# Value halves of the U rounds of batches 0 and 1 in the PSUM banks of the output tiles

## The chip, the cores and the metric

The kernel runs on one core of one Trainium2 chip. The metric is the device time of the whole kernel in microseconds, as the median of several runs; lower is better. A run counts as slow when it lies over 1.5% above the fastest of the same kernel; all runs compared here are fast ones unless it is said otherwise. The runs were made in several batches, each on another chip, with the kernel before measured beside them every time. The granted clock is the share of TensorE's full clock that the chip's throttle let through. The profile is one further look at one execution; its span is some 1.8 us below the timed figure, and its times are counted from the span's start.

## The reference, cut to what matters

```python
# attention with 32 memory slots per head, 8 batches, 8 heads, 576 tokens
a = softmax(phi, over tokens)
k_m, v_m = a^T k, a^T v                       # per head: 32 x 64
attn = softmax(q k_m^T / 8)                   # 576 x 32
x = (attn v_m), heads side by side            # 4608 x 512
# gated feed-forward, 512 -> 1536 -> 512
out = (silu(x w_gate) * (x w_val)) w_out
```

The kernel never forms x. Since x w = attn (v_m w), it first multiplies the small v_m into the weights. That product is U, one for gates and one for values, per batch and per block of 512 columns ("chunk").

## The kernel before: the parts that matter

The kernel uses eight banks of PSUM, the memory to which TensorE writes its results; each tile takes one bank until ScalarE or VectorE has read it out. Six form the pool `ps`, from which nearly every tile comes; two form the pool `po` for output tiles (and for the dummy matmuls of `warm`).

```python
ps = ctx.enter_context(tc.tile_pool(name="ps", bufs=6, space=bass.MemoryType.PSUM))
po = ctx.enter_context(tc.tile_pool(name="po", bufs=2, space=bass.MemoryType.PSUM))
```

A U round computes one or two "parts" (in a full round the gate half and the value half of a chunk), each into two banks, and evacuates them to SBUF, alternately by ScalarE ("a") and VectorE ("v").

```python
def u_round(b, parts, evac):
    banks = []
    for which, c, halves in parts:
        ...
        p = [ps.tile([128, 2, HC], FP32, tag="b", name=f"p_u{g}")... for g in range(NG)]
        for w in which:
            for i in range(NP):
                for g in range(NG):
                    nc.tensor.matmul(p[g][32 * i:32 * i + 32, o:o + n], lhsT=kTs[b]..., rhs=W[w, c]...)
        ...
    for (t, p, r), e in zip(banks, evac):
        ...   # ScalarE: copy or activation; VectorE: tensor_copy or tensor_scalar
```

A gate and value slot computes a gate tile (two matmuls), has ScalarE take its silu, computes the value tile of the slot before (two matmuls), and has VectorE multiply the two. In batches 0 and 1 the slots and U rounds are in this order:

```python
run([u_half(1, (0, 1), 0, 1, "av")] + g0[4:8] + g1[4:5])
for c in range(1, NCH):                     # two chunks, so four full U rounds
    s = 8 * c
    run([u_item(0, c)] + g1[s - 3:s] + g0[s:s + 5])
    run([u_item(1, c)] + g0[s + 5:s + 8] + g1[s:s + 5])
run(g1[-3:])
flush_mul()
backlog = out_list(0) + out_list(1)         # po's banks: unused from the last warm to here
```

The softmax here doesn't subtract the row's maximum and nothing guards it: scores larger than these inputs give would overflow.

Of the kernel before, what the change touches and what calls it, by code (L numbers as in the profile page):

```python
# [9 lines left out]
FP32 = mybir.dt.float32  # L10
# [4 lines left out]
def kernel(  # L15
# [40 lines left out]
    ps = ctx.enter_context(tc.tile_pool(name="ps", bufs=6, space=bass.MemoryType.PSUM))  # L56
    po = ctx.enter_context(tc.tile_pool(name="po", bufs=2, space=bass.MemoryType.PSUM))
# [57 lines left out]
    HC = CH // 2  # L115
# [249 lines left out]

    scaled = set()

    def u_round(b, parts, evac):


        banks = []
        for which, c, halves in parts:
            w0, w1, h0, h1 = which[0], which[-1] + 1, halves[0], halves[-1] + 1
            n = (h1 - h0) * HC
            p = [
                ps.tile([128, 2, HC], FP32, tag="b", name=f"p_u{g}").rearrange("p a f -> p (a f)")
                for g in range(NG)
            ]
            for w in which:
                o = (w - w0) * n  # L380
                for i in range(NP):
                    for g in range(NG):
                        nc.tensor.matmul(  # L383
                            p[g][32 * i:32 * i + 32, o:o + n],
                            lhsT=kTs[b][64 * g:64 * g + 64, 2, 32 * i:32 * i + 32],
                            rhs=W[w, c][64 * g:64 * g + 64, h0:h1, i],
                            start=True,
                            stop=True,
                            tile_position=(64 * g, 32 * i),
                        )  # L390
            for g in range(NG):
                if (b, c, g) not in Us:
                    Us[b, c, g] = upool.tile([128, 2, 2, HC], BF16, tag=f"U{c}{g}", name="t_U")
                if len(which) == 1:
                    dst = Us[b, c, g][:, h0:h1, w0]
                else:
                    dst = Us[b, c, g][:, h0]
                src = p[g][:, 0:(w1 - w0) * n].rearrange("p (a f) -> p a f", f=HC)
                banks.append((dst, src, rSs[b][:, g, 0] if b in scaled else None))
        for (t, p, r), e in zip(banks, evac):  # L400
            if e == "a":
                if r is None:
                    nc.scalar.copy(out=t, in_=p)  # L403
                else:
                    nc.scalar.activation(out=t, in_=p, func=AF.Copy, scale=r)
            elif r is None:
                nc.vector.tensor_copy(out=t, in_=p)  # L407
            else:
                nc.vector.tensor_scalar(out=t, in0=p, scalar1=r, scalar2=None, op0=ALU.mult)
# [5 lines left out]
    def flush_mul(n=None):  # L415
        for _ in range(len(pend) if n is None else n):
            pend.pop(0)()
# [16 lines left out]
    def gv_gate(b, s):  # L434

        jf, r = s // 2, s % 2
        if b % 2 == 0 and r == 0:
            hts[b // 2, jf] = hpool.tile([128, 2 * S], BF16, tag=f"h{jf}", name="t_h")
        gate = gv_half(b, s, 0)
        sg = work.tile([128, HALF], BF16, tag="sg", bufs=8, name="t_sg")  # L440
        nc.scalar.activation(out=sg, in_=gate, func=AF.Silu)  # L441
        col = (b % 2) * S + r * HALF
        dst = hts[b // 2, jf][:, col:col + HALF]

        def mul():
            val = gv_half(b, s, 1)
            nc.vector.tensor_tensor(out=dst, in0=sg, in1=val, op=ALU.mult)  # L447

        pend.append(mul)
# [97 lines left out]
            lambda g=g, n=n: q_T(b, g, n, evac[2 * g + n]) for g in range(NG) for n in range(2)  # L547
        ]

    def u_item(b, c, evac="avav"):  # L550

        return lambda: u_round(b, (((0,), c, (0, 1)), ((1,), c, (0, 1))), evac)

    def u_half(b, which, c, half, evac):

        return lambda: u_round(b, ((which, c, (half,)),), evac)

    def u_three(b):

        u_round(b, (((0,), 0, (0, 1)), ((1,), 0, (0, 1)), ((0,), 1, (0, 1))), "avavav")  # L560
# [4 lines left out]
    def run(items):  # L565
        for x in items:
            x()
# [13 lines left out]
    def gv_slots(b):  # L581
        return [lambda s=s: gv_slot(b, s) for s in range(2 * NJF)]
# [78 lines left out]

    g0, g1 = gv_slots(0), gv_slots(1)
    run([u_half(0, (0,), 0, 0, "av"), u_half(1, (0,), 0, 0, "av")])
    warm(6)
    for s in range(4):
        gv_gate(0, s)
    run([u_half(0, (1,), 0, 0, "va"), u_half(1, (1,), 0, 0, "va")])
    for s in range(2):
        gv_gate(1, s)
    flush_mul(3)  # L670
    run([u_half(0, (0, 1), 0, 1, "va")])
    flush_mul(2)
    run(g1[2:4])
    run([u_half(1, (0, 1), 0, 1, "av")] + g0[4:8] + g1[4:5])
    for c in range(1, NCH):
        s = 8 * c
        run([u_item(0, c)] + g1[s - 3:s] + g0[s:s + 5])
        run([u_item(1, c)] + g0[s + 5:s + 8] + g1[s:s + 5])
    run(g1[-3:])
    flush_mul()  # L680
    backlog = out_list(0) + out_list(1)
# [7 lines left out]
    for b in range(2, B):  # L689
# [30 lines left out]
        g = gv_slots(b)  # L720
# [3 lines left out]
        if last:  # L724
            streams += [([u_item(b, 2)], 5, 6)]
# [55 lines left out]
```

## Time and profile before

The kernel took 249.45 us (249.39 to 249.8). The stages that the argument touches:

| stretch of the profile, us | what runs | what it waits for |
|---|---|---|
| 27 to 35.7 | half U rounds, first slots | U evacuations as data |
| 35.75 to 57.0 | four full U rounds, eight slots after each but the last, eleven after that | 0.3 us per round: banks in the second to fourth, mostly a load in the first (shown below) |
| 57.0 to 79 | output tiles of batches 0 and 1, K and V sums of batch 2 | nothing of note |
| 86.1 | K and V sums of batch 3 | nothing: V of batch 3 had landed at 85.5 |
| to 243.9 | batches 3 to 7 and the last output tiles | next to nothing |

A line of the chain of waits reads: start, length, engine, tile that is written, source line, number of instructions. A line of the timeline adds the operation and, in brackets, the engine's idle time before it and what ended that. The prediction below shows the lines of before.

### The profile page before, as it was taken

The page shows a single profiled execution, that of the slowest core. Times are in us where ns is not written, and L with a number is a line of the kernel's source. Part 1 is how long each engine was busy: PE and PEld are TensorE (multiplying, and loading weights), DVE is VectorE, ACT ScalarE, POOL GpSimd, SP SyncE. Part 2 cuts the span into 40 slices and gives each one's busy share as a digit, 9 for nine tenths or more (in the row PEclk, how much of TensorE's full clock was granted, in tenths as well). Part 3 has the DMA queues.
Part 4 walks back from the last instruction along what each step waited for, and adds up shares of the span by engine and source line. Part 5 has one row for each costly group of instructions (what it writes and reads, how often), then busy time and mean ns, then how long its engine had stood idle before and what let it go on. Part 6 is the DMA issues. An engine that isn't in the chain of part 4 may idle for free.

```text
span 247.6 us, 6587 instructions
## 1 busy us (share of the span) xinstructions
PE 237.5 (96%) x2573; PEld 152.3 (61%) x2600; DVE 158.9 (64%) x337; ACT 165.2 (67%) x356; POOL 54.5 (22%) x85
## 2 busy tenths in 40 slices
PE   7999999999999999999999999999999999999993
PEld 7966666665544765467645666476546655467543
DVE  0046599994437788479846778478846877587420
ACT  2447888886077667966896577966896577676201
POOL 8423455000060004060405420090007000000000
PEclk9999999999999999999999999999999999999998
DMA  7999999999689976996996599289425311310143
GB/s 182 206 204 203 196 197 201 233 199 198 134 158 248 231 168 95 207 282 145 125 243 191 94 175 249 91 119 196 94 51 123 65 42 42 87 42 0 45 128 85
DMA packets 49167, 37.00 MB, mean 149 GB/s; under 512 B 15984, under 2 KB 43888, under 8 KB 49136
## 3 DMA queue, kind: packets, MB, share of 16 engines
q0 software_dynamic: 27632, 22.42, 57.0%
q1 hardware_dynamic: 20496, 13.37, 22.7%
q10 hardware_dynamic: 1008, 0.79, 1.2%
q8 instruction: 20, 0.33, 0.5%
q14 instruction: 11, 0.09, 0.1%
HBM read 42.47 MB, written 9.44 MB: 210 GB/s over the span
## 4 chain that ended last, share of the span: by engine, by line
PE 87%; DMA 8%; POOL 2%; issue 2%; ACT 0%; POOLq 0%
PE p_oo L483 36%; PE p_g L425 20%; PE p_v L425 19%; DMA t_kv<-in_v_dram 8%; PE p_u L383 6%; PE p_kv L183 2%; PE p_oo L514 1%; POOL t_q L93 1%; POOL t_kv L81 1%; PE p_g L351 1%; PE p_v L351 1%; PE p_g L331 1%; PE p_vT L290 0%; PE p_kv L203 0%; PE p_oo L588 0%
## 5 line engine op out<-in xcount | busy, mean ns | idle before, releaser
L483 PE MATMUL p_oo<-WO,t_h 128*128 128x512 bf16 x393 | 101.6, 379 | 3.0 <-issue 2.9
L441 ACT ACTIVATE t_sg<-p_g 128x288 bf16<-128x288 f32 x192 | 76.9, 413 | 31.6 <-PE p_g L425 24.2
L447 DVE TENSOR_TENSOR t_h<-t_sg,p_v 128x288 bf16<-128x288 bf16 x192 | 84.3, 453 | 18.9 <-PE p_v L425 14.8
L425 PEld LDWEIGHTS <-t_U 128*128 128x128 bf16 x768 | 74.3, 98 | 30.7 <-issue 2.3
L425 PE MATMUL p_g<-t_A,t_U 128*128 128x288 bf16 x384 | 77.5, 286 | 0.4
L425 PE MATMUL p_v<-t_A,t_U 128*128 128x288 bf16 x384 | 76.8, 286 | 0.0
L483 PEld LDWEIGHTS <-t_h 128*128 128x128 bf16 x420 | 39.6, 98 | 41.0 <-issue 6.0
L495 DVE COPY t_o<-p_oo 128x512 f32<-128x512 f32 x27 | 18.6, 690 | 31.4 <-PE p_oo L483 31.3
L407 DVE CAST t_U<-p_u 128x512 bf16<-128x512 f32 x42 | 26.7, 684 | 6.8 <-PE p_u L383 6.8
L403 ACT CAST t_U<-p_u 128x512 bf16<-128x512 f32 x30 | 15.8, 592 | 8.9 <-PE p_u L383 8.9
L493 ACT COPY t_o<-p_oo 128x512 f32<-128x512 f32 x8 | 4.7, 589 | 19.9 <-PE p_oo L483 10.6
L100 POOL DMA_DIRECT2D t_q<-in_q_dram x6 | 4.7, 782 | 59.3 <-DMA t_qT<-t_q 58.5
L588 PE MATMUL p_oo<-bones 128*128 128x128 bf16 x198 | 15.7, 244 | 1.5 <-DVE bones L603 1.5
L383 PE MATMUL p_u<-W,t_kT 64*32 64x512 bf16 (+1 forms) x416 | 15.7, 365 | 0.1
L153 ACT ACTIVATE t_ephi<-t_phi 96x768 bf16<-96x768 f32 x16 | 12.5, 843 | 4.1 <-DMA t_phi<-in_phi_dram 4.1
L588 PEld LDWEIGHTS <-bones 128*128 128x128 bf16 x198 | 13.9, 111 | 2.1 <-DVE bones L603 1.5
L166 POOL COPY t_mark<-t_A 1x1 bf16<-1x1 bf16 x4 | 0.7, 181 | 55.7 <-DVE t_A L360 55.7
L341 ACT ACTIVATE t_E<-p_g 128x288 bf16<-128x288 f32 x16 | 6.6, 412 | 8.5 <-PE p_v L331 7.9
L360 DVE TENSOR_TENSOR t_A<-t_E,t_lz 128x576 bf16<-128x576 bf16 x16 | 11.5, 750 | 0.5 <-ACT t_lz L355 0.5
L355 ACT ACTIVATE t_lz<-t_lz 128x576 f32<-128x576 f32 x16 | 10.9, 684 | 0.5
L170 POOL TENSOR_TENSOR t_es<-t_es,t_ephi 96x256 f32<-96x256 f32 x16 | 10.7, 669 | 1.3
L383 PEld LDWEIGHTS <-t_kT 64*32 64x32 bf16 x416 | 4.8, 89 | 8.8 <-issue 7.3
(58 smaller groups left out, 167.9 us busy)
## 6 DMA issues: line engine op xcount, KB each, us to landing
t_kv<-in_k_dram POOLq DMA_DIRECT2D x8, 576.0 KB, 9.3
t_kv<-in_v_dram POOLq DMA_DIRECT2D x8, 576.0 KB, 14.2
out_dram<-t_o SPq DMA_DIRECT2D x23, 192.0 KB, 2.5
t_phi<-in_phi_dram POOLq DMA_DIRECT2D x6, 576.0 KB, 15.3
t_q<-in_q_dram POOLq DMA_DIRECT2D x6, 576.0 KB, 7.4
out_dram<-t_o SPq DMA_DIRECT2D x24, 128.0 KB, 2.5
W<-in_moe_w_gate_dram POOLq DMA_DIRECT2D x6, 256.0 KB, 12.9
W<-in_moe_w_val_dram POOLq DMA_DIRECT2D x6, 256.0 KB, 11.9
```

Source lines behind the costliest of these rows:

```text
L153: nc.scalar.activation(out=t[:, :, g].rearrange("p j i m -> p i j m"), in_=src[:, g], func=AF.Exp)
L355: nc.scalar.activation(out=lz, in_=lz, func=AF.Exp, scale=-1.0)
L360: nc.vector.tensor_tensor(out=a, in0=es.pop((b, g)), in1=lzs.pop((b, g)), op=ALU.mult)
L383: nc.tensor.matmul(p[g][32 * i:32 * i + 32, o:o + n], lhsT=kTs[b][64 * g:64 * g + 64, 2, 32 * i:32 * i + 32], rhs=W[w, c][64 * g:64 * g + ...
L403: nc.scalar.copy(out=t, in_=p)
L407: nc.vector.tensor_copy(out=t, in_=p)
L425: nc.tensor.matmul(p[:, 0:HALF], lhsT=Us[b, c, g][:, o // 2, which, 128 * (o % 2):128 * (o % 2 + 1)], rhs=atts[b, g][:, r], start=(g == 0) ...
L441: nc.scalar.activation(out=sg, in_=gate, func=AF.Silu)
L447: nc.vector.tensor_tensor(out=dst, in0=sg, in1=val, op=ALU.mult)
L483: nc.tensor.matmul(mine["p"], lhsT=hts[c, jf][:, 128 * u:128 * (u + 1)], rhs=WO[jf], start=(jf == 0), stop=(jf == NJF - 1),)
L495: nc.vector.tensor_copy(out=t_o, in_=mine["p"])
L588: nc.tensor.matmul(p[:, 0:128], lhsT=bones, rhs=bones, start=True, stop=True)
```

## The change

Its intent: two banks are idle while the six of the ring are short. Let the value half of each full U round, and a whole part of three half rounds, use them.

```diff
-    def u_round(b, parts, evac):
+    def u_round(b, parts, evac, spare=-1):
...
-        for which, c, halves in parts:
+        for n_part, (which, c, halves) in enumerate(parts):
+            pool, tag = (po, "o") if n_part == spare else (ps, "b")
...
-                ps.tile([128, 2, HC], FP32, tag="b", name=f"p_u{g}").rearrange("p a f -> p (a f)")
+                pool.tile([128, 2, HC], FP32, tag=tag, name=f"p_u{g}").rearrange(
...
-    run([u_half(0, (1,), 0, 0, "va"), u_half(1, (1,), 0, 0, "va")])
+    run([u_half(0, (1,), 0, 0, "va"), u_half(1, (1,), 0, 0, "va", 0)])
...
-    run([u_half(0, (0, 1), 0, 1, "va")])
+    run([u_half(0, (0, 1), 0, 1, "va", 0)])
...
-    run([u_half(1, (0, 1), 0, 1, "av")] + g0[4:8] + g1[4:5])
+    run([u_half(1, (0, 1), 0, 1, "av", 0)] + g0[4:8] + g1[4:5])
...
-        run([u_item(0, c)] + g1[s - 3:s] + g0[s:s + 5])
-        run([u_item(1, c)] + g0[s + 5:s + 8] + g1[s:s + 5])
+        run([u_item(0, c, spare=1)] + g1[s - 3:s] + g0[s:s + 5])
+        run([u_item(1, c, spare=1)] + g0[s + 5:s + 8] + g1[s:s + 5])
```

(The new argument is handed through `u_item` and `u_half`; those lines are cut.)

More of the change, by code (lines that the diff above doesn't have):

```diff
@@ L375, in u_round @@
             p = [
-                ps.tile([128, 2, HC], FP32, tag="b", name=f"p_u{g}").rearrange("p a f -> p (a f)")
+                pool.tile([128, 2, HC], FP32, tag=tag, name=f"p_u{g}").rearrange(
+                    "p a f -> p (a f)"
+                )
                 for g in range(NG)
@@ L548, in q_items, with u_item, u_half @@
         ]
-    def u_item(b, c, evac="avav"):
-        return lambda: u_round(b, (((0,), c, (0, 1)), ((1,), c, (0, 1))), evac)
-    def u_half(b, which, c, half, evac):
-        return lambda: u_round(b, ((which, c, (half,)),), evac)
+    def u_item(b, c, evac="avav", spare=-1):
+        return lambda: u_round(b, (((0,), c, (0, 1)), ((1,), c, (0, 1))), evac, spare)
+    def u_half(b, which, c, half, evac, spare=-1):
+        return lambda: u_round(b, ((which, c, (half,)),), evac, spare)
     def u_three(b):
```

## The prediction

> **What bounds the kernel now.** I read, in this order, the page's busy rows, the chain of work that ended last, that chain in order of time around the changed rounds, and the timeline of ScalarE and VectorE beside it.
>
> ```profile
> PE 237.5 (96%) x2573; PEld 152.3 (61%) x2600; DVE 158.9 (64%) x337; ACT 165.2 (67%) x356; POOL 54.5 (22%) x85
> PE 87%; DMA 8%; POOL 2%; issue 2%; ACT 0%; POOLq 0%
> ```
>
> TensorE holds the chain for 87% of the span. In order of time the only long piece that isn't TensorE is a load of V before 25.8 us; from there to 241 us the chain is TensorE alone. So a microsecond that TensorE stops losing near 30 to 57 us shortens the run by as much, unless a later transfer holds it up. "96% busy" hides the losses, because a matmul's end is modelled; the chain in order of time shows them as lengthened pieces. Here is the second of the four full U rounds (start, length, what):
>
> ```profile
> 40.45 0.24 PE p_v L425 x2
> 40.69 0.56 PE p_u L383 x16
> 41.25 0.35 PE p_g L425 x2
> 41.60 0.24 PE p_v L425 x2
> 41.84 0.40 PE p_g L425 x2
> 42.24 0.25 PE p_v L425 x2
> 42.49 0.33 PE p_g L425 x2
> 42.82 0.30 PE p_v L425 x2
> 43.12 0.25 PE p_g L425 x2
> ```
>
> A pair of gate or value matmuls takes 0.245 us undisturbed. After the round the pieces are 0.35, 0.40, 0.33 and 0.30: excesses of 0.105, 0.155, 0.085 and 0.055. The rounds at 45.57 and 50.45 repeat this to 0.01 us. To see who causes each, I set it beside the other two engines (start, length, engine, line):
>
> ```profile
> 41.10 0.69 ACT L405 ACTIVATE t_U<-p_u,t_rS 128x512 bf16<-128x512 f32 x1 [0.20 <-PE p_u L383]
> 41.17 0.74 DVE L409 TENSOR_SCALAR t_U<-p_u,t_rS 128x512 bf16<-128x512 f32 x1
> 41.69 0.68 ACT L405 ACTIVATE t_U<-p_u,t_rS 128x512 bf16<-128x512 f32 x1
> 41.84 0.74 DVE L409 TENSOR_SCALAR t_U<-p_u,t_rS 128x512 bf16<-128x512 f32 x1
> 42.26 0.71 ACT L441 ACTIVATE t_sg<-p_g 128x288 bf16<-128x288 f32 x2
> 42.49 0.81 DVE L447 TENSOR_TENSOR t_h<-t_sg,p_v 128x288 bf16<-128x288 bf16 x2
> ```
>
> The pool of six banks is a ring: each tile takes the bank of the tile six before it. A U round takes four banks, U0 to U3, and the tiles that follow are g1, v1, g2, v2, g3, v3. Six back from g2, v2, g3, v3 stand U0, U1, U2, U3. The first ScalarE evacuation ends at 41.10 + 0.69 = 41.79 and g2 starts at 41.84 on the timeline; the second ends at 41.69 + 0.68 = 42.37 and g3 starts at 42.42. So two waits are bank waits with 0.05 us from release to start. VectorE's second evacuation ends at 42.58 and v3 starts at 42.72: a release by VectorE costs about 0.14.
>
> The first of these rounds differs:
>
> ```profile
> 35.82 0.34 PE p_u L383 x8
> 36.16 0.07 issue
> 36.23 0.41 PE p_u L383 x8
> 36.64 0.35 PE p_g L425 x2
> ```
>
> Undisturbed, 16 of these matmuls take 0.56 as above; here 0.82. The second half waits for U3's bank, whose VectorE product starts at 35.55 and ends at 36.01. Later one value piece is 0.28, an excess of 0.035. That is 0.30 again.
>
> **What the Trainium skill says.** "Perfetto Trace Analysis", section Optimization Strategy: the same gap repeating on the engine that should be saturated can mean that SBUF or PSUM ran out for the next tile. This trace agrees: 0.295 us, three times alike. The same page, section Matmul Optimizations, asks that all 8 PSUM banks be used; here two are idle from the last warm-up matmul (27.9) to the first output matmul (57.0). "PSUM — Partial Sum Buffer", section PSUM bank collisions, has it that two engines must not touch one bank and quadrant at once and that software must guard it; so a bank comes back only when its whole evacuation is over, which the 0.05 us after ScalarE's end bears out. "TensorE: Matmul & The Clock Gate", Part 3, The mechanism: a weight load overlaps running matmuls only where its row group differs. That fits the 0.105 on g1: no bank is missing there (its bank's silu ended at 40.90), yet the load of full-height weights starts 0.25 us after the last small one. I take 0.105 as staying.
>
> **The change, part by part.** No instruction is added or removed: the same 128 matmuls (4.4 us), 14 ScalarE and 14 VectorE evacuations (8.1 and 8.9 us), in the same order. Only banks move. In each full round the value half (U2, U3) goes to the two output banks, and the ring gives up two banks instead of four; in three half rounds near 29 to 33 us a whole part goes there. Their last owner is four or five microseconds back in the full rounds and 1.9 us in the half rounds, where its evacuations are over (30.4 before the 30.9 round, 32.4 before 32.8). So no new wait at U.
>
> The ring after a full round now reads, six back: g1 and v1 from two slots before, g2 and v2 from the slot before, g3 from U0, v3 from U1, g4 from g1, v4 from v1. Worked through with the times above, U starting at 40.62:
> - g1 41.18 and v1 41.44, as now.
> - g2 needs the silu that ended at 40.90: it goes at 41.69, not 41.84. v2 at 41.93.
> - g3 needs U0, free at 41.79: it goes at 42.18. v3 needs U1, free at 41.91: 42.42.
> - g4 would go at 42.67 but needs g1's silu, which stands behind two evacuations: 42.26 + 0.41 + 0.05 = 42.72. A wait of 0.05.
> - v4 would go at 42.96 but needs the product that frees v1's bank, behind VectorE's two: 42.49 + 0.44 + 0.14 = 43.07. A wait of 0.10.
> - g5 43.31, v5 43.56; their releases (about 42.97, and 43.30 + 0.14) are in time.
>
> Now v5 starts at 43.69. So of 0.295 only about 0.13 is regained; the rest comes back as a wait for silu and product, because the evacuations themselves take 1.3 us of each engine and haven't moved. Back to back, products come every 0.37 us against TensorE's 0.49 per slot, so both engines catch up before the next round, and each round repeats it: 3 x 0.13 = 0.39.
>
> In the first full round, U ends without the 0.26 wait, but its evacuations started at once anyway (36.22 and 36.30) and then silu at 37.38 and product at 37.75 follow with no gap. v4 then goes near 38.24 and v5 near 38.73, against 38.82 now: about 0.1. In the half rounds the chain has 0.36, 0.34 and 0.36 for U and the 0.105 after it, and no excess beyond; only the second gate near 29.7 waits some 0.06, and the value after it needs ScalarE's evacuation as data (ends 30.02, starts 30.07). I count 0.05. Sum: 0.05 + 0.1 + 0.39 = 0.54 us.
>
> Does it survive? K and V of batch 3 are loaded behind Q of batch 2, which is limited by transfer and not by TensorE (issued 42.3, landed 20.6 later). V is issued at 70.07 and takes 15.4, so it lands at 85.5; TensorE starts those sums at 86.08. The slack is 0.6, just above the gain. The transposed Q of batch 2 lands at 68.0 and is wanted at 69.8. So nearly all of 0.54 should reach the end: 249.45 - 0.54 = 248.9.
>
> **The rivals.**
> - All excess goes: 4 x 0.295 + 0.1 = 1.28, so 248.2. For it: bank waits are what the diff removes. Against it: the evacuations keep silu and product late, and the V load caps the gain near 0.6.
> - The wait merely moves: v4 waits longer. If a VectorE release costs 0.22, as at 36.01 to 36.23, v4 goes at 43.15 and a round gains 0.05, in all about 0.25: 249.2. With an earlier landing deadline missed as well, 249.45. For it: VectorE is busy 4.70 of the 4.88 us of a period. Against it: much of that busy time is products paced by TensorE at 0.49.
> - The shared banks hurt: a U tile holds up the first output tile, or an extra semaphore instruction lands on TensorE's queue (51 ns each, 5 now at U). The last U evacuation in them ends near 52.3, the first output matmul is at 57.0, so I give this at most 0.3 us: 249.75.
>
> **Range and chances.** The second rival's and the first's ends give 248.2 to 249.4; the three times of before spread over 0.4, so I widen the upper end to 249.6. Two per cent is 5.0 us; the excess at all changed rounds together is 1.3 us, and nothing changed can cost 5 us. So within 2% is almost certain.
>
> **What would show it right or wrong.** Right: in the chain in order of time the pieces after a full U round read 0.35, 0.24, near 0.25, 0.25, 0.25, 0.25, then about 0.3 and 0.35 at the fourth gate and value; the first full round's U takes 0.56 in one piece; the first output matmul starts near 56.5 instead of 57.04; ScalarE and VectorE have the same counts and busy times; the K and V sums of batch 3 start near 85.6. Wrong: the fourth slot shows no wait and output starts at 55.8 (first rival), output starts at 56.5 but the end hasn't moved (V's landing, or a transfer after it, took the gain back), or a U round itself is longer than 0.56.

## The result

The changed kernel took 249.09 us (248.88 to 249.19, four runs), beside 249.42 us for the kernel before on the same chip: 0.33 us less. The ratio is 0.9982, 95% interval 0.9965 to 1.0: within 2%. A ratio here is the mean time of one kernel's fast runs over that of the other's in the same rounds, so it isn't quite the ratio of the medians quoted. The time lies within the predicted range. When the same kernel was run again later, it took 248.92 us against 249.55 (ratio 0.9977, interval 0.9964 to 0.9989). The first interval reaches 1.0, so it alone doesn't show a gain; the second does.

The busy row of the page after, to be set beside the first one of the prediction:

```profile
PE 239.5 (97%) x2600; PEld 150.7 (61%) x2600; DVE 158.5 (64%) x337; ACT 165.0 (67%) x356; POOL 54.5 (22%) x85
```

Instruction counts are the same. The program of before has 2600 matmuls too; 27 records are missing from its trace, which accounts for its lower TensorE figure. So this row says nothing about the gain; the chain in order of time does. First the second full round of the changed kernel:

```profile
40.83 0.56 PE p_u L386 x16
41.38 0.35 PE p_g L428 x2
41.73 0.24 PE p_v L428 x2
41.98 0.24 PE p_g L428 x2
42.23 0.24 PE p_v L428 x2
42.47 0.24 PE p_g L428 x2
42.72 0.24 PE p_v L428 x2
42.96 0.30 PE p_g L428 x2
43.26 0.30 PE p_v L428 x2
```

The 0.40, 0.33 and 0.30 of before are gone. The 0.35 on the first gate stays. At the fourth gate and value there are two new pieces of 0.30: the wait has come back in part, at the place where the prediction put it. From this round's start to the next one's took 45.57 - 40.69 = 4.88 us before; now it takes 45.52 - 40.83 = 4.69. That is 0.19 us regained per round, and the next two rounds do the same.

The first full round, in the same view:

```profile
25.86 10.40 DMA W<-in_moe_w_val_dram
36.26 0.14 issue
36.39 0.41 PE p_u L386 x8
```

The chain now runs through a load of value weights that lands at 25.86 + 10.40 = 36.26. The second half of the U matmuls follows it, at 36.39, and before it followed at 36.23. Whatever was won up to here is lost to this load, and 0.16 us more.

So the output phase starts at 56.61 instead of 57.04: 0.43 us earlier. But the last piece of the chain, ScalarE's last copy, starts at 243.63 instead of 243.93: 0.30 us earlier. The rest goes at the K and V sums of batch 3. Their denominators start at 85.27, 0.44 before the 85.71 of the kernel before, but the sums themselves start at 85.78 instead of 86.08, because V was issued at 70.25, took 15.49 us and landed at 85.74.

### The profile page after: what moved, and what is told of

Its sections match the earlier page's. It is cut to its first block, busy times and chain, and to the rows that moved or that the text cites. A ratio compares the mean times of both kernels' runs of the same rounds, so it can differ in the third digit from the quotient of the medians.

```text
span 247.4 us, 6614 instructions
## 1 busy us (share of the span) xinstructions
PE 239.5 (97%) x2600; PEld 150.7 (61%) x2600; DVE 158.5 (64%) x337; ACT 165.0 (67%) x356; POOL 54.5 (22%) x85
## 4 chain that ended last, share of the span: by engine, by line
PE 75%; DMA 20%; POOL 3%; issue 1%; ACT 0%; POOLq 0%
PE p_oo L486 32%; PE p_g L428 17%; PE p_v L428 17%; DMA t_kv<-in_v_dram 14%; PE p_u L386 4%; DMA W<-in_moe_w_val_dram 4%; DMA t_qT<-t_q 2%; PE p_kv L183 2%; PE p_oo L517 1%; POOL t_q L93 1%; POOL t_kv L81 1%; PE p_g L351 0%; PE p_v L351 0%; PE p_g L331 0%; POOL t_q L100 0%
## 5 line engine op out<-in xcount | busy, mean ns | idle before, releaser
L486 PE MATMUL p_oo<-WO,t_h 128*128 128x512 bf16 x420 | 108.6, 379 | 0.0
L591 PE MATMUL p_oo<-bones 128*128 128x128 bf16 x198 | 14.6, 234 | 1.5 <-DVE bones L606 1.5
L591 PEld LDWEIGHTS <-bones 128*128 128x128 bf16 x198 | 12.8, 106 | 2.2 <-DVE bones L606 1.5
L408 ACT ACTIVATE t_U<-p_u,t_rS 128x512 bf16<-128x512 f32 (+1 forms) x14 | 8.3, 628 | 2.9 <-PE p_u L386 2.9
## 6 DMA issues: line engine op xcount, KB each, us to landing
t_phi<-in_phi_dram POOLq DMA_DIRECT2D x6, 576.0 KB, 15.2
```

Of the source, the lines that this page charges most:

```text
L486: nc.tensor.matmul(mine["p"], lhsT=hts[c, jf][:, 128 * u:128 * (u + 1)], rhs=WO[jf], start=(jf == 0), stop=(jf == NJF - 1),)
L591: nc.tensor.matmul(p[:, 0:128], lhsT=bones, rhs=bones, start=True, stop=True)
```

## The experiments

My theory after the first result had three parts. First, in a full round 0.19 of the 0.295 us of bank waits go, and 0.11 comes back because silu and product stand behind the evacuations. Second, the landing of the value weights near 36.2 swallows what is gained before it. Third, the landing of V near 85.0 to 85.7 swallows part of what is left. The rivals: the half rounds carry a share to the end; the first full round's wait was for a bank (so the prediction had it); ScalarE and VectorE limit the rounds whatever the banks; something later sets the end.

Every run was correct. "Output" is the start of the first output matmul in the chain, "sums" that of the sums of batch 3 with their wait for V where the profile shows one, "last" the start of the chain's last piece.

| kernel | output | sums (wait) | last | time, us | ratio |
|---|---|---|---|---|---|
| before | 57.04 | 86.08 | 243.93 | 249.42 to 249.55 | 1 |
| after, first time | 56.61 | 85.78 | 243.63 | 249.09 | 0.9982 |
| half_only | 57.03 | 86.08 | 243.92 | 249.41 | 1.0002 |
| full_only | 56.36 | 85.41 | 243.25 | 248.82 | 0.9977 |
| after_again | 56.27 | 85.75 (0.38) | 243.60 | 248.92 | 0.9977 |
| before_wlate | 56.87 | 85.91 | 243.75 | 249.35 | 0.9990 |
| after_wlate | 56.07 | 85.99 (0.81) | 243.83 | 249.17 | 0.9977 |
| before_kvlate | 57.01 | 87.25 | 244.72 | 250.45 | 1.0030 |
| after_kvlate | 56.45 | 86.69 | 248.97 | 255.72 | 1.0245 |
| after_kv2 | 56.79 | 86.32 | 243.68 | 249.00 | 0.9980 |
| after_wlate_kv3 | 56.05 | 86.29 | 242.94 | 248.56 | 0.9963 |
| ring8 | 56.38 | 85.44 | 243.29 | 248.77 | 0.9973 |
| ring8_wlate_kv3 | 55.76 | 86.00 | 242.65 | 248.37 | 0.9953 |
| the same, again | 56.14 | 86.38 | 243.03 | 248.35 | 0.9952 |

Times differ by 0.3 us and more within one kernel, so I lean on the profiles for the cause and on the ratios only for the size. The 95% intervals are about 0.0012 to either side in most runs. A profile is one execution too: two of the changed kernel start output 0.34 us apart. But two stretches of the chain repeat almost exactly, and they carry the argument:

- From the start of the second full round to output: 16.33 to 16.35 us in the four kernels without the change in the full rounds, 15.76 to 15.78 in the seven profiles with it, 15.46 in the three with the ring of eight. So the three later rounds gain 0.57 and 0.88 us whenever they run. What else moves output lies before that round.
- From output to the last piece: 186.88 to 186.91 us wherever the sums of batch 3 and 4 don't wait. Where those of batch 3 wait it is longer: by 0.13 (after, first time), 0.44 (after_again, wait 0.38) and 0.87 (after_wlate, wait 0.81).

### half_only: the half rounds alone

```diff
-        run([u_item(0, c, spare=1)] + g1[s - 3:s] + g0[s:s + 5])
-        run([u_item(1, c, spare=1)] + g0[s + 5:s + 8] + g1[s:s + 5])
+        run([u_item(0, c)] + g1[s - 3:s] + g0[s:s + 5])
+        run([u_item(1, c)] + g0[s + 5:s + 8] + g1[s:s + 5])
```

> Only the three half rounds use the output banks; the four full rounds are as before. Theory (whatever is gained before the first full round is lost again to the landing of value weights near 36.1 to 36.3 us): the half rounds bring the start of the first full round from 35.75 to about 35.6 us, but its second half still starts at 36.2 to 36.4; pieces of 0.40 and 0.33 after the later full rounds stay; the output phase starts at 57.0 to 57.2; time within 0.1 us of before, ratio 0.9995 to 1.0005. Rival (the half rounds carry their share to the end): output starts at 56.85 to 56.9 and the time falls by 0.15 us.

Nothing was gained: output started at 57.03, ratio 1.0002 (0.999 to 1.0014). The chain around the first full round:

```profile
36.20 0.06 issue
36.26 0.41 PE p_u L386 x8
```

The second half of U started at 36.26, no earlier than before. The weights landed at 25.97 + 10.2 = 36.17. The profile names another releaser, a product of VectorE that ended at 36.20. Here are the products, first of the kernel before, then of half_only in two neighbouring windows:

```profile
35.55 0.83 DVE L447 TENSOR_TENSOR t_h<-t_sg,p_v 128x288 bf16<-128x288 bf16 x2
...
35.38 0.81 DVE L450 TENSOR_TENSOR t_h<-t_sg,p_v 128x288 bf16<-128x288 bf16 x2
35.74 0.44 DVE L450 TENSOR_TENSOR t_h<-t_sg,p_v 128x288 bf16<-128x288 bf16 x1
```

The named product is that of the last value tile before the round. By the count of the ring, U3 takes the bank of the value tile before that one, whose product ended at 35.38 + 0.44 = 35.82. And in the kernel before, the last product ended at 35.55 + 0.83 = 36.38, after U's second half had started (36.23), so U doesn't wait for it. That leaves the weights. By the profile, the rival that the half rounds carry 0.15 us to the end is out; the interval of the ratio is too wide to say so alone.

### full_only: the full rounds alone

```diff
-    run([u_half(0, (1,), 0, 0, "va"), u_half(1, (1,), 0, 0, "va", 0)])
+    run([u_half(0, (1,), 0, 0, "va"), u_half(1, (1,), 0, 0, "va")])
...
-    run([u_half(0, (0, 1), 0, 1, "va", 0)])
+    run([u_half(0, (0, 1), 0, 1, "va")])
...
-    run([u_half(1, (0, 1), 0, 1, "av", 0)] + g0[4:8] + g1[4:5])
+    run([u_half(1, (0, 1), 0, 1, "av")] + g0[4:8] + g1[4:5])
```

> Only the four full rounds put their value half into the output banks; the half rounds are as before. Theory: everything that the whole change gained: the pieces after the second to fourth full round read 0.35, 0.24, 0.24, 0.24, 0.24, 0.24, 0.30, 0.30, 0.19 us gained per round, output starts at 56.4 to 56.7, sums of batch 3 start at 85.6 to 85.8, time 0.3 us below before (ratio 0.9988). Rival (half rounds carry a share): output starts at 56.8 or later and the gain is 0.2 us or less.

All of the gain is here: 248.82 us, ratio 0.9977. The round period is 45.28 - 40.59 = 4.69, as in the whole change. In the first full round the bank wait is now impossible, since the value half has banks of its own. The weight loads of TensorE in the timeline (in brackets, the idle time and what ended it) show the wait nonetheless:

```profile
36.16 0.11 PEld L386 LDWEIGHTS <-t_kT 64*32 64x32 bf16 x8 [0.32 <-DMA W<-in_moe_w_val_dram]
```

The second half waits for the value weights (landed at 26.02 + 10.1 = 36.12) and starts at 36.16, just 0.07 earlier than in the kernel before. U takes 0.77 us instead of 0.82: of the 0.26 lost, 0.05 went with the bank. In this execution V came earlier as well (issued at 69.68, 15.3 us later landed at 84.98), so the sums didn't wait and the whole 0.68 us of output's start reached the end.

### after_again: the changed kernel once more

> The changed kernel once more, unaltered. Theory (transfers that land at slightly different times from run to run set how much of the gain is kept: value weights near 36.1 to 36.3 us, V of batch 3 at 85.0 to 85.75): times between 248.75 and 249.2, median near 248.95; this profile's output start may be 56.45 to 56.65, and the sums of batch 3 start at 85.4 to 85.8. Rival (the half rounds cost something lasting, so that the change is slower than its full rounds alone): median 249.05 to 249.15 again, at least 0.2 above the 248.82 of the full rounds alone.

248.92 us, as the theory had it, and the first result isn't a lasting cost of the half rounds: this is 0.1 us from full_only, with overlapping runs (248.83 to 249.08 against 248.73 to 249.04). The profile shows the third part of the theory outright. Output started at 56.27, 0.34 earlier than in the first profile of the same program, because this time the second half of the first full round got going at 36.06. Yet the last piece started at 243.60, as in the first profile:

```profile
85.75 0.85 PE L183 MATMUL p_kv<-t_kv,t_ephi 96*32 96x128 bf16 x48 [0.38 <-DMA t_kv<-in_v_dram]
```

### before_wlate and after_wlate: the first full round one slot later

The first full round is moved behind one more slot, so that its weights have landed. Nothing else moves. For the kernel before:

```diff
-    run([u_half(1, (0, 1), 0, 1, "av")] + g0[4:8] + g1[4:5])
+    run([u_half(1, (0, 1), 0, 1, "av")] + g0[4:8] + g1[4:6])
...
-        run([u_item(0, c)] + g1[s - 3:s] + g0[s:s + 5])
+        run([u_item(0, c)] + g1[s - (2 if c == 1 else 3):s] + g0[s:s + 5])
```

> The kernel before, with its first full round one slot later. It tells what that round's wait of 0.26 us was. If it was the value weights' landing (near 36.1): U takes 0.56 to 0.6 in one piece, and the four pieces after it then show the 0.155, 0.085 and 0.055 of the other full rounds, so that output starts within 0.1 of 57.04 and the time is 249.4 to 249.6. If it was the wait for U3's bank, as the prediction has it: U still takes 0.75 to 0.85 with the gap in its middle, one slot later.

```profile
36.13 0.56 PE p_u L383 x16
...
37.29 0.40 PE p_g L425 x2
37.68 0.24 PE p_v L425 x2
37.93 0.33 PE p_g L425 x2
38.26 0.30 PE p_v L425 x2
```

U takes 0.56 in one piece, and behind it stand the three bank waits of the other rounds. By itself this doesn't separate the two releasers, since the product that frees U3's bank came earlier too (0.14 us after U's start instead of 0.26). With half_only and full_only it does: the binding wait in the first full round of the kernel before was the weights' landing (26.04 + 10.1 = 36.14), and the bank, free at 36.01, came just before it. Output started at 56.87, 0.17 earlier; but in this execution the first U round had already started 0.17 earlier (26.82 against 26.99), so the move gained nothing: one wait stepped into the place of the other. The time was 249.35.

For the changed kernel the same move was run:

> The change, with the first full round one slot later, so that its value weights have landed. Theory (the weights' landing took what the half rounds and the first full round gain): its 16 U matmuls take 0.56 in one piece with no wait for the weights, the pieces after it show about 0.1 us of waits as in the other full rounds, and output starts 0.15 to 0.3 us earlier than in the change: 56.2 to 56.4; the end keeps part of it, 248.7 to 249.0. Rival (the wait was for the bank and has just moved): U still 0.7 to 0.8 long and output start unaltered.

U took 0.59, output started at 56.07, earlier than forecast, and yet the last piece started at 243.83. In the timeline of TensorE:

```profile
84.74 0.44 PE L203 MATMUL p_kv<-ones,t_ephi 96*128 96x1 bf16 x12
85.99 0.85 PE L183 MATMUL p_kv<-t_kv,t_ephi 96*32 96x128 bf16 x48 [0.81 <-DMA t_kv<-in_v_dram]
```

The denominators were done, and the sums waited 0.81 us for V, issued at 70.00 and landed 15.9 us later. Output 0.97 us earlier than in the kernel before, the end 0.10 earlier: the V load had taken back the rest. The theory's forecast for the end, 248.7 to 249.0, was therefore too good for the median (249.17); the five runs spread from 248.47 to 249.31.

### after_kvlate and before_kvlate: the sums of batch 3 later, a try that failed

```diff
-                (kv_items(3, lambda: (u_item(2, 2)(), run(take(2)))), 10, 14),
+                (kv_items(3, lambda: (u_item(2, 2)(), run(take(2)))), 12, 15),
```

> The whole change, and in batch 2 the K and V sums of batch 3 are placed some 1.3 us later in TensorE's order, so that V's landing near 85.5 to 85.8 us can't hold them up. Theory (V's landing took 0.13 of the 0.43 us won by 57 us): the sums start near 86.9 with no wait for the V load, and the last piece of the chain starts 0.43 us before that of the kernel before: 243.5 instead of 243.63; time 0.43 below before (ratio 0.9983). Rival (something else, later, sets the end): the end stays 0.30 below before although the sums no longer wait.

> Control: the kernel before, with the sums of batch 3 placed 1.3 us later as in the run beside it. Theory: before had 0.3 to 0.6 us of room between V's landing and the sums, so nothing was waiting and nothing is gained: 249.4, ratio 0.9995 to 1.0005. Rival (the later place is of use by itself, or costs something): a change of 0.15 us or more.

Both expectations failed: 255.72 us and 250.45 us (two of the control's six runs, at 255.6 and 258.5, count as slow and are left out; their clocks, 0.993 and 0.987, and times are like those of after_kvlate's runs, 253.3 to 256.6, which all count as fast, so they may have taken the same course; they have no profile). The edit did more than I had meant. Two output matmuls go with the sums, and moving them took the store that hangs on them past the transposition of Q of batch 3 in SyncE's queue. Here is that transposition, first in the kernel before:

```profile
90.76 3.28 SPq L106 DMA_TRANSPOSE t_qT<-t_q  x1
```

and in after_kvlate, with the sums of batch 4 and a stretch of the windows view (from:to, length, then busy time of each engine, then the granted clock):

```profile
80.72 7.93 SPq L106 DMA_TRANSPOSE t_qT<-t_q  x1
...
115.69 0.85 PE L183 MATMUL p_kv<-t_kv,t_ephi 96*32 96x128 bf16 x48 [3.39 <-DMA t_kv<-in_v_dram]
...
116.00:120.00 4.00, 3.69 (x66) 2.09 (x56) 2.44 (x6) 1.89 (x4) 0.00 (x0) 0.64 0.77 109
```

The transposition went out ten microseconds earlier and occupied the queue for 7.93 us instead of 3.28. V of batch 4 is issued once it has landed, at 99.95 instead of 97.65 in the changed kernel, took 15.7 us instead of 13.5, and the sums of batch 4 waited 3.39 us. In the control they waited 0.75 us, and the last piece started 0.79 later than before. After the wait the clock was lower: over the four microseconds that followed, 0.64 was granted, over the next four 0.94. An estimate from these: 4 x 0.36 + 4 x 0.06 = 1.7 us, with the wait 5.1, and the end is 248.97 - 243.63 = 5.3 us later than in the changed kernel's first profile. (Counted from output it is 5.6 us above the 186.9 of the undisturbed profiles, so about 0.5 stays unexplained.) That the transposition took longer because loads were under way at the time is argued, not shown. "TensorE: Matmul & The Clock Gate", section HAM oscillation, warns of gaps above some 3.4 us on TensorE; this one gap, of just about that length (3.39 us) and with a clock of 0.64 after it, fits. The pair says nothing about V of batch 3; it only showed that V of batch 4 has little room too.

### after_kv2: the sums one slot later, the queues' order kept

```diff
-                (kv_items(3, lambda: (u_item(2, 2)(), run(take(2)))), 10, 14),
+                (kv_items(3, lambda: (u_item(2, 2)(), run(take(2)))), 11.35, 13.55),
```

> The change, with the K and V sums of batch 3 one gate and value slot (0.49 us) later, the stores' queue in unaltered order (the earlier try moved the Q transposition ahead of a store and so delayed V of batch 4). Theory: V's landing can't hold the sums up, so the whole gain at the start of the output phase (0.4 to 0.6 us) reaches the end: 248.8 to 249.0, and the sums show no wait. Rival (V of batch 4, with some 1.4 us of room, or something later becomes the limit): the end is no better than the change's 249.1.

249.00 us: no better than the change itself. The profile is of little use for the question: this time an earlier load of value weights landed at 31.52 (at 16.93 + 13.8 = 30.73 in the kernel before) and held up a half round, so that the first full round started at 36.34 and output at 56.79:

```profile
16.60 14.92 DMA W<-in_moe_w_val_dram
31.57 0.30 PE p_u L386 x8
```

The sums didn't wait, and all 0.25 us that output had won reached the end (243.68). Inconclusive by itself.

### after_wlate_kv3: both loads out of the way

```diff
 against after_wlate:
-                ([lambda: load_qT(3)], 12, 12),
-                (kv_items(3, lambda: (u_item(2, 2)(), run(take(2)))), 10, 14),
+                ([lambda: load_qT(3)], 12.7, 12.7),
+                (kv_items(3, lambda: (u_item(2, 2)(), run(take(2)))), 12.1, 14.1),
```

> The change with both suspected limits moved out of the way: the first full round one slot later (as in the earlier run, where the output phase started at 56.07 but the sums of batch 3 waited 0.81 us for V and the end gained nothing), and those sums two slots and one output matmul, 1.19 us, later, the stores' and loads' queues in unaltered order. Theory: output starts at 56.0 to 56.3, the sums show no wait for V, and the last piece of the chain starts as much earlier as output does, 0.7 to 1.0 below before (242.9 to 243.2); time 248.5 to 248.8. Rival (a later transfer, V of batch 4 with some 1 us of room, takes it back): sums of batch 4 show a wait and the end is 243.4 or later.

It differs from after_wlate only in where the sums of batch 3 stand, and in the load of Q of batch 3, which moves with them to keep its place. Output started at the same time (56.05 against 56.07), but the sums no longer waited:

```profile
86.29 0.85 PE L183 MATMUL p_kv<-t_kv,t_ephi 96*32 96x128 bf16 x48
```

The last piece started at 242.94 against 243.83. So some 0.87 us, counted from output, had been lost at V's landing there. How much of it the move saves isn't shown: in this execution V also landed 0.8 us earlier (69.42 + 15.7 = 85.1 against 85.9), and would hardly have held up the sums in their old place. Time 248.56, ratio 0.9963 (0.9951 to 0.9975).

### ring8: one ring of eight banks

Instead of a fixed share for U tiles, U, gate and value tiles take the eight banks in turn. (A wait can't simply be removed here without a race; giving a tile an older bank is the way to remove it.)

```diff
 against the kernel before:
+    ring = {"n": None}
+
+    def bank(shape, name):
+        if ring["n"] is None:
+            return ps.tile(shape, FP32, tag="b", name=name)
+        ring["n"] += 1
+        pool, tag = (po, "o") if ring["n"] % 8 in (6, 7) else (ps, "b")
+        return pool.tile(shape, FP32, tag=tag, name=name)
...
-                ps.tile([128, 2, HC], FP32, tag="b", name=f"p_u{g}").rearrange("p a f -> p (a f)")
+                bank([128, 2, HC], f"p_u{g}").rearrange("p a f -> p (a f)")
...
-        p = ps.tile([128, CH], FP32, tag="b", name=f"p_{'gv'[which]}")
+        p = bank([128, CH], f"p_{'gv'[which]}")
...
+    ring["n"] = 0          # before the first slots
...
-        run([u_item(1, c)] + g0[s + 5:s + 8] + g1[s:s + 5])
+        run([u_item(1, c)] + g0[s + 5:s + 8])
+        if c == NCH - 1:
+            ring["n"] = None
+        run(g1[s:s + 5])
```

> Instead of giving the two output banks to U tiles only, U, gate and value tiles of batches 0 and 1 go round all eight banks as one ring (until the last full round's first three slots are over, so that the output phase finds its banks free). Theory (a tile eight back is always free in time: the fourth gate waits for U2, free at 42.4, not for a silu): the pieces after the second to fourth full round read 0.35 and then 0.24 throughout, 0.295 us gained per round instead of 0.19, output starts at 56.1 to 56.3 (the change 56.4 to 56.6), time 248.6 to 248.9. Rival (ScalarE and VectorE behind the round are the limit whatever the banks): 0.30 pieces stay somewhere and the gain per round is 0.19 as in the change.

```profile
40.92 0.56 PE p_u L392 x16
41.48 0.35 PE p_g L434 x2
...
43.06 0.24 PE p_g L434 x2
43.30 0.24 PE p_v L434 x2
```

The fourth gate and value take 0.24 too, and the period is 45.51 - 40.92 = 4.59 us: 0.29 regained per round. So ScalarE and VectorE aren't the limit of a round; the 0.11 that the change leaves is a bank wait. Output started at 56.38, later than expected, because in this execution the first full round's second half didn't start before 36.49. (The weights landed at 25.95 + 10.4 = 36.35; as in half_only the profile names the product of the last value tile, ended at 36.46, which isn't the owner of U3's bank.) Time 248.77, ratio 0.9973.

### ring8_wlate_kv3: all three together

The edits of ring8, before_wlate and after_wlate_kv3 together.

> The ring of eight banks with the same two moves. Theory: no bank wait in any full round, output starts at 55.7 to 56.0, and most of 1.1 us reaches the end: 248.2 to 248.6, the fastest of all. Rival (V of batch 3 or 4 is the limit again): the sums wait and the time stays at 248.7 to 249.0.

> The fastest kernel once more, because one of its six runs took 254.0 us against 248.05 to 248.76 for the other five. If that was a disturbed run: all runs here lie between 248.0 and 248.9. If the kernel itself has a second course (for instance a load that misses its deadline, as in the first try at moving the sums): again one run in about five near 252 to 256.

248.37 us, ratio 0.9953 (0.994 to 0.9965), and the second time 248.35, ratio 0.9952. The last piece started at 242.65 and 243.03; in the second profile the same early load of value weights as in after_kv2 landed late again (16.83 + 14.45 = 31.28). One of the eleven runs took 254.0 us at a granted clock of 0.993 and counts as slow; it didn't come again in the repeat (248.13 to 248.55), but its cause is open. after_kvlate's profiled run, with its missed load, had the same clock and took 254.5, so a missed load is as possible as a disturbance. This version beats both kernels, by 1.1 to 1.2 us against before.

## Why the prediction was right or wrong

The time was predicted at 248.9 and came at 249.09 and, the second time, 248.92. The steps:

- **What bounds the kernel.** Right. TensorE's chain carries the time; where no load stood in between, what output gained reached the end in full (0.68 of 0.68 in full_only).
- **The ring of six and the waits at g2, g3 and v3.** Right. Given other banks, these three waits vanished in the second to fourth full round.
- **The wait that comes back at the fourth slot.** The mechanism was right and the size somewhat off. Two pieces of 0.30 stand exactly at g4 and v4. The term "a release by VectorE costs about 0.14" was too large: in the changed kernel the product ends at 42.63 + 0.44 = 43.07 and v4 starts at 43.15, so 0.08. Hence 0.19 regained per round instead of 0.13, for three rounds 0.57 instead of 0.39. The ring of eight shows that what remains is indeed a wait for banks.
- **The first full round.** Wrong. The step "The second half waits for U3's bank" took the releaser that fitted in time. The bank was free at 36.01, the value weights landed at 36.14, and the start was at 36.23. In the changed kernel U didn't take "0.56 in one piece". half_only has the bank free 0.44 us before the second half starts; full_only shows the same wait without any possible bank wait, released by the load; before_wlate shows 0.56 without a gap once the weights are there. The term "about 0.1" for this round is in truth a deadline: no less than the landing allows. In two profiles of the changed kernel the weights landed at 36.26 and 35.91, and the second half started at 36.39 and 36.06.
- **The half rounds.** "I count 0.05": they gained more by themselves (from the start of the first U to that of the first full round 26.99 to 35.75 before, 27.08 to 35.70 after: 0.14), and nothing of it lasted, because the weights' landing comes next. half_only: ratio 1.0002.
- **Does it survive?** The step "nearly all of 0.54 should reach the end" had the right obstacle and too much trust in its slack. V landed at 85.5 before and at 85.74 in the first profile after, where the sums needed it at some 85.65 (0.38 after their denominators' start). It held them by 0.13 us there, 0.38 in after_again and 0.81 in after_wlate. Of the 0.43 us won by the output phase in the first profile 0.30 reached the end.
- **The rivals.** "All excess goes" is refuted for the change and is what the ring of eight does in the second to fourth round. "The wait merely moves" is right for 0.11 of 0.295 us. Nothing showed that the shared banks hurt: U's semaphore instructions on TensorE's queue stayed at 5.
- **The 0.105 at the first gate.** It stayed, as the prediction took it. The reason given there, that a weight load overlaps running matmuls only where its row group differs, is not shown: in the slots the loads are of full height as well, 98 ns each, and yet a pair of matmuls with its two loads takes 0.245 us, so they overlap. No run removed the 0.105; its cause is open.

The errors offset each other: too little per round, too much for the first round, too little for the V load. That the total came so near is in part luck, all the more as the landings shift the time from run to run.

## What to carry to other kernels

Spare PSUM banks helped most here in the ring from which the waiting tiles come: as a fixed share for one kind of tile they regained two thirds of the waits of a round, as part of one ring all of them. Before counting on a gain, list the loads that land shortly before they are needed downstream of it: each such slack, less its spread from run to run, is a ceiling on what can reach the end. And where two releasers fit a wait within a tenth of a microsecond, the trace of one kernel may not tell them apart, and the releaser that the profile names can be the wrong one (half_only); a run that removes one of them helps more.

## What the Trainium skill lacked or had wrong

- "Perfetto Trace Analysis", section Matmul Optimizations, asks that all eight banks be used, and the page's section Matmuls that groups rotate through them; no page that I read compares a fixed share with one ring: with two banks reserved for U tiles a round regained 0.19 us, in one ring of eight 0.29 us of 0.295.
- No page that I read gives the time from a bank's release to the waiting matmul: here 0.05 us after ScalarE's end, 0.08 to 0.14 after VectorE's.
- No page that I read gives the spread of a load's landing between executions of one program: here in two profiles of the changed kernel such a load took 10.4 us both times but was issued, and so landed, 0.35 us apart (36.26 and 35.91). Over the profiles of all kernels here V of batch 3 was issued between 69.42 and 70.25 and took 15.2 to 15.9 us.
